# Full 128-by-128 products in the search for the experts' thresholds, and attention's state products moved behind its results

## The chip, the core and the metric

The kernel runs on one core of a Trainium2 chip. The metric is the device time of one execution in microseconds (us), the median of several runs. The core has a matrix engine (TensorE: PE for its products, PEld for the loading of the stationary operand), VectorE (DVE), ScalarE (ACT), GpSimd (POOL) and DMA queues. A product's form is written as rows*columns of the array that it uses: `128*48` takes a contraction over 128 rows and 48 output partitions. The shape behind it is that of the moving operand.

## What is computed

Three stages follow each other: a linear attention with a decaying state, a dense two-layer network with a squared ReLU, and a routed network of eight experts with a fixed capacity of N/E = 384 tokens each.

```python
for t in range(S):                                   # attention, B=4, H=8, S=768, D=48
    state = alpha[:, :, t, :, None] * state + einsum('bhd,bhe->bhde', k[:, :, t], v[:, :, t])
    y[:, :, t] = einsum('bhd,bhde->bhe', q[:, :, t], state)
x = y.transpose(0, 2, 1, 3).reshape(3072, 384)
h = maximum(x @ w_in, 0); x = h * h @ w_out          # dense, d_ff = 2048
logits = x @ w_gate                                  # routed, 8 experts, d_ff = 1024
# (token, expert) pairs in falling order of logit: a token takes the expert if both are still free
out[mask] = maximum(x[mask] @ w1[e], 0) @ w2[e]
```

## The kernel before

**Attention and the dense network.** The 3072 tokens are 24 chunks of 128 (six to each of the four batch rows), and three chunks make a unit of 384 for the dense network. Eight units run one behind the other, each in 16 steps `f`: `moe_a` (9 products into `ph`, line 388), the square on ACT, DVE and POOL (`moe_ev`, lines 393 to 404), and two steps later `moe_b` (9 products into three `p2` banks, line 416). Between these steps stand the pieces of one attention chunk each: `psc` (scores, line 252, form 48*128), `pn` (transposes, 292), and in the last piece the state's products `pu` (line 303, form 128*48) and the result's `py`, which are first those with the decayed state `sad` (line 270, form 112*128) and then those with the masked scores `Pt` (line 273, form 128*48). `update` makes `pu`, and DVE adds it to the state (line 309); the next chunk's `sad` is made of it on POOL. `result` makes `py`, and ACT copies it out (line 276). Chunks 0 and 1 run before the first unit, chunk 2 (`late`) has its update last. A chunk that begins a batch row has no `sad`, one that ends it (`last`) has no update. That leaves fourteen chunks from chunk 3 on with all three: 3, 4, 7 to 10, 13 to 16 and 19 to 22.

In the first unit DVE also converts the dense network's weights (`narrow`, lines 348 to 352), and the order on every engine is the program's. From the second unit on a scheduler places the instructions of the other engines by their readiness.

**The search.** An expert's threshold is found in five rounds (`it` 0 to 4) of a 32-way search. Each round is a chain between PE and DVE: `cm` (line 861, comparisons), six products `pc` (869, 128*128), a copy `rc` (872), four products `pb` with the constant `same` (882), a comparison `full` (885), one product with the constant `later` (887), its sum `n` (896), and the next `cm`. A last product `pz` (908) gives the counts. `same` has 32 columns for each product (form 128*32), `later` has 32 rows (32*128), and `pz` takes 32 rows (32*128): the 32 threshold candidates lie on 32 partitions. There are seven such searches, `k` = 0 to 6. Search 0 runs among the dense network's last unit (line 671), search 1 while the first expert's weights are prepared, and searches 2 to 6 inside the experts' products.

**The experts.** Each expert has eight steps `s`: `layer1` (9 products, line 988, with ACT's and DVE's lines 996 and 997 behind it) and `layer2` (three times 3 products, line 1006). A hand-written table (`STEADY`, `EXTRA` and others) says what is put before, between and behind them in each step: a piece of the search, a gather, `expert_x` (transposes, line 961, whose results ACT and DVE copy in 962 and 963), or the split of the next expert's weights into two parts (951 on ACT, 953 on POOL or DVE). What stands in the table is the order of the program, and of every engine's queue.

Of the kernel before, what the change touches and what calls it, by code (L numbers as in the profile page):

```python
# [7 lines left out]
F32 = mybir.dt.float32  # L8
F32R = mybir.dt.float32r
BF = mybir.dt.bfloat16  # L10
F16 = mybir.dt.float16
I32 = mybir.dt.int32
AF = mybir.ActivationFunctionType
OP = mybir.AluOpType
# [6 lines left out]
E, F2 = 8, 1024  # L21
# [3 lines left out]
CPU = 3  # L25
# [7 lines left out]
T = 32  # L33
G = 128 // T
ITERS = 5
# [50 lines left out]
def moe_kernel(ctx: ExitStack, tc: tile.TileContext, akq, v, w_in, w_out, w_gate, w1, w2, out,  # L86
               dbg=None, force=False):
    nc = tc.nc
    pe, dve, act, pool, sp = nc.tensor, nc.vector, nc.scalar, nc.gpsimd, nc.sync
    consts = ctx.enter_context(tc.tile_pool(name="consts", bufs=1))  # L90
# [40 lines left out]
    ident = consts.tile([128, 128], F32, name="ident")  # L131
    dve.tensor_scalar(ident, jp, 0.0, None, op0=OP.is_equal)
    ones = consts.tile([128, 128], F32, name="ones")
# [3 lines left out]
    scratch = consts.tile([128, 1], F32, name="scratch")  # L137
# [31 lines left out]
    for i in range(2):  # L169
        t = ap_.tile([112, NP, 128], F32, name=f"sad{i}")  # L170
# [6 lines left out]
    def iota(shape, pattern, base=0, cm=0, name="io"):  # L177
        t = consts.tile(shape, F32, name=name)
        pool.iota(t, pattern=pattern, base=base, channel_multiplier=cm, allow_small_or_imprecise_dtypes=True)
        return t  # L180

    ioe = iota([128, E], [[1, E]], base=ID0, name="ioe")
    iop = iota([128, 1], [[0, 1]], cm=1, name="iop")
# [2 lines left out]
    pool.iota(iopc[:, :, 1], pattern=[[1, NCH]], base=0, channel_multiplier=0, allow_small_or_imprecise_dtypes=True)  # L186
    onesb = consts.tile([128, 128], BF, name="onesb")
    trim = consts.tile([128, 128], BF, name="trim")
    later = consts.tile([T, 128], BF, name="later")
    same = consts.tile([128, 128], F16, name="same")  # L190
    iopw = iota([128, 1], [[0, 1]], base=-128 * ID0, cm=1, name="iopw")
    sel = consts.tile([16, E], F32, name="sel")

    def late_consts():
        pool.memset(onesb, 1.0)
        dve.tensor_scalar(trim, jp, 0.0, -1.0, op0=OP.is_gt, op1=OP.add)
        dve.tensor_scalar(later, ones[0:T], iop[0:T], 0.5, op0=OP.mult, op1=OP.is_gt)
        dve.tensor_copy(same, ident)
        dve.tensor_scalar(sel, jp[0:16, 0:E], -float(E), None, op0=OP.is_equal)
        dve.tensor_tensor(sel, sel, ident[0:16, 0:E], op=OP.add)  # L200

# [10 lines left out]
    def attn(ch, tags="aaaaa"):  # L212
# [3 lines left out]
        last = c == S // C - 1  # L216
# [31 lines left out]
        late = ch == CPU - 1  # L248
        for p in (3, 0, 1, 2) if late else range(NP):
            for j in range(2):  # L250
                o = 64 * j
                pe.matmul(psc[j][:, p * 128:(p + 1) * 128], kt[o:o + D, p], qt[o:o + D, p],  # L252
                          start=True, stop=True)
# [44 lines left out]
        def update():  # L298
            pu = bank(next(tag), "pu")
            for p in range(NP):  # L300
                for j in range(2):
                    o = 64 * j
                    pe.matmul(pu[o:o + D, p * 64:p * 64 + D], kn2[:, p, j], vn[:, 2 * p + j],  # L303
                              start=True, stop=True)
            for j in range(2):
                o = 64 * j
                src = v4(pu[o:o + D, 0:256])[:, :, 0:D]
                if c:
                    dve.tensor_tensor(state[o:o + D], src, sa[o:o + D, :, o:o + D], op=OP.add)  # L309
                else:  # L310
                    (act.copy if ch == 0 else dve.tensor_copy)(state[o:o + D], src)

        if not (last or late):
            update()
        result(0, NP - late)
        if late:
            update()
        yield "o"

# [370 lines left out]
    sm, sm_stack = open_pool("route", "right")  # L690
# [8 lines left out]
    cap = sm.tile([128, E], F32, name="cap")  # L699
# [7 lines left out]
    pool.iota(iot[:, 0], pattern=[[1, T]], base=0, channel_multiplier=0, allow_small_or_imprecise_dtypes=True)  # L707
    for i in range(1, ITERS):
        act.activation(iot[:, i], iot[:, i - 1], AF.Copy, scale=1.0 / T)
    iol = sm.tile([T, 1], F32, name="iol")  # L710
    act.activation(iol, iop[0:T], AF.Copy, scale=float(T) ** (1 - ITERS))
    ioslot = sm.tile([128, CAP], F32, name="ioslot")
    pool.iota(ioslot, pattern=[[1, CAP]], base=-int(OFF), channel_multiplier=0, allow_small_or_imprecise_dtypes=True)
    IDX, XG, RW = {}, {}, {}
# [116 lines left out]
    def search(k):  # L831
# [20 lines left out]
        n, at = None, zero24[:, 0:1]  # L852
        for it in range(ITERS):

            pc = bank("a", "pc")
            thr = iot[:, 0]
            if it:
                thr = pc[:, G * E:G * E + T]
                dve.tensor_scalar(thr, iot[:, it], n, at, op0=OP.add, op1=OP.add)
            cm = sm.tile([128, NCH, T], BF, name="cm", bufs=2)  # L860
            dve.tensor_tensor(cm, m2[:, :, None].to_broadcast([128, NCH, T]),
                              thr[:, None, :].to_broadcast([128, NCH, T]), op=OP.is_ge)
            if it == 0:
                oh = sm.tile(eb, BF, name="oh", bufs=2)
                dve.tensor_tensor(oh, L, m[:, :, None].to_broadcast(eb), op=OP.is_equal)
            yield

            for c in range(0, NCH, G):
                pe.matmul(pc[:, 0:G * E], cm[:, c:c + G].rearrange("p c t -> p (c t)"),
                          oh[:, c:c + G].rearrange("p c e -> p (c e)"), start=c == 0, stop=c == NCH - G)  # L870
            rc = sm.tile([128, G * E], F16, name="rc", bufs=2)
            dve.tensor_copy(rc, pc[:, 0:G * E])
            if it == 1:
                ee = sm.tile(eb, F32, name="ee", bufs=1)
                dve.tensor_tensor(ee, oh, ioe[:, None, :].to_broadcast(eb), op=OP.mult)
            if it == 2:
                ei = sm.tile([128, NCH], F32, name="ei", bufs=2)
                dve.tensor_reduce(ei, ee, axis=AX.X, op=OP.add)
            yield
            pb = bank("a", "pb")  # L880
            for g in range(G):
                pe.matmul(pb[0:T, 0:E], same[:, g * T:(g + 1) * T], rc[:, g * E:(g + 1) * E], start=g == 0,
                          stop=g == G - 1)
            full = sm.tile([T, E], BF, name="full", bufs=2)
            dve.tensor_tensor(full, pb[0:T, 0:E], cap[0:T], op=OP.is_ge)
            yield
            pe.matmul(pb[:, E:2 * E], later, full, start=True, stop=True)
            if it == 1:
                at = n
            elif 1 < it < ITERS - 1:  # L890
                at2 = sm.tile([128, 1], F32, name="at", bufs=2)
                dve.tensor_scalar(at2, at, n, None, op0=OP.add)
                at = at2
            n0, n = n, sm.tile([128, 1], F32, name="n", bufs=4)
            steps = sm.tile([128, E], F32, name="steps", bufs=1)
            dve.tensor_scalar(steps, pb[:, E:2 * E], float(T) ** -it, None, op0=OP.mult, op1=OP.max, accum_out=n)
            yield

        hi = sm.tile([128, 1], F32, name="hi", bufs=2)
        dve.tensor_scalar(hi, n, n0, at, op0=OP.add, op1=OP.add)  # L900
        taken = sm.tile([T, E], F32, name="taken", bufs=2)
        dve.scalar_tensor_tensor(taken, n[0:T].to_broadcast([T, E]), iol, pb[0:T, 0:E], op0=OP.is_equal, op1=OP.mult)
        a = pb[:, 2 * E:2 * E + NCH]
        dve.tensor_scalar(a, m2, hi, None, op0=OP.is_ge)
        dve.copy_predicated(aid, a.bitcast(mybir.dt.uint32), ei)
        yield
        pz = bank("a", "pz")
        pe.matmul(pz[:, 0:E], ones[0:T], taken, start=True, stop=True)
        cl = sm.tile([128, E], F32, name="cl", bufs=2)
        dve.tensor_tensor(cl, cap, pz[:, 0:E], op=OP.subtract)  # L910
        cz = sm.tile([128, E], F32, name="cz", bufs=2)
# [379 lines left out]
```

## Time and profile before

| | |
|---|---|
| median of three runs | 868.7 us (868.61 to 869.08) |
| the profiled execution | 867.91 us |
| its span in the trace | 865.7 us |
| PE busy | 813.1 us, 94% of the span |
| DVE, ACT, POOL busy | 498.1, 337.6, 366.3 us |
| granted clock of PE, mean | 0.975 |

The profiled execution's time is 2.2 us more than its span, which is what lies around the trace. The trace is read here by its timeline: a row stands for a run of equal instructions on one engine, and the difference of the starts of two neighbouring rows is what the first of them took of the engine, since PE's own ends are modelled. Tenths of a microsecond in such differences are the subject of this case.

### The profile page before, as it was taken

What the parts mean: (1) busy time and instruction counts of PE and PEld (TensorE: products, weight loads), DVE (VectorE), ACT (ScalarE), POOL (GpSimd) and SP (SyncE); (2) the same over time, 40 slices, a digit from 0 to 9 for tenths busy, and PEclk for the clock granted to TensorE, in tenths of its full rate; (3) what the DMA queues carried; (4) which work ended last, traced back from release to release, by engine and by line L of the source; (5) the groups of instructions that cost most, each with busy time, mean ns of one, the idle gap of its engine ahead of it and who ended that gap; (6) DMA issues with size and microseconds to landing.
All of it is one profiled execution on the core that took longest, in us unless ns stands there. A gap on an engine that the chain in (4) does not pass through costs nothing.

```text
span 865.7 us, 14472 instructions
## 1 busy us (share of the span) xinstructions
PE 813.1 (94%) x5752; PEld 755.0 (87%) x5752; DVE 498.1 (58%) x1149; ACT 337.6 (39%) x615; POOL 366.3 (42%) x350
## 2 busy tenths in 40 slices
PE   7699999999999999999999999986999999999994
PEld 6588898999999999999999998875887888889993
DVE  7999884444444434435434213476876877876730
ACT  2265464233234233233233334213435536536620
POOL 2456562343342343343242344125457567572511
PEclk9899899999999999999999999996999999999997
DMA  8545322112112112112100000031432522513500
GB/s 257 158 160 188 125 76 79 42 49 69 43 49 70 42 49 70 42 49 74 64 23 28 1 23 13 15 143 49 173 129 74 201 97 105 192 69 141 199 31 30
DMA packets 21626, 75.54 MB, mean 87 GB/s; under 512 B 3137, under 2 KB 10178, under 8 KB 19634
## 3 DMA queue, kind: packets, MB, share of 16 engines
q0 software_dynamic: 5520, 34.61, 10.9%
q1 hardware_dynamic: 11682, 25.72, 9.4%
q10 hardware_dynamic: 4352, 14.24, 5.5%
q8 instruction: 46, 0.75, 0.4%
q14 instruction: 26, 0.21, 0.1%
HBM read 63.84 MB, written 9.54 MB: 85 GB/s over the span
## 4 chain that ended last, share of the span: by engine, by line
PE 76%; DVE 11%; ACT 5%; DMA 3%; issue 2%; POOL 0%; SPq 0%; POOLq 0%; DVEq 0%; ACTq 0%
PE ph L388 22%; PE p L416 20%; PE ph L988 9%; PE py L1006 7%; ACT wbuf L951 3%; PE psc L252 3%; DVE wbuf L953 3%; PE py L273 2%; PE p L671 2%; PE py L270 2%; DMA akq<-in_akq_dram 2%; DMA w1s<-in_moe_w_dram,wi 2%; PE pn L292 1%; DVE hl L997 1%; PE pu L303 1%
## 5 line engine op out<-in xcount | busy, mean ns | idle before, releaser
L388 PE MATMUL ph<-xT,wbuf 128*128 128x384 f32 x1152 | 228.3, 342 | 7.2 <-DVE wbuf L459 5.0
L388 PEld LDWEIGHTS ph<-xT,wbuf 128*128 128x128 f32 x1152 | 206.1, 190 | 10.9 <-DVE wbuf L459 6.0
L416 PE MATMUL p<-wbuf,hl 128*128 128x392 f32 (+1 forms) x1008 | 204.1, 346 | 0.0
L400 DVE SCALAR_TENSOR_TENSOR s<-ph,s 128x384 f32<-128x384 f32 x112 | 62.3, 557 | 223.4 <-ACT s L393 222.9
L416 PEld LDWEIGHTS p<-wbuf,hl 128*128 128x128 f32 x1008 | 177.8, 189 | 4.0 <-issue 3.0
L404 POOL TENSOR_TENSOR hl<-s,hl 128x384 fp32r<-128x384 f32 x96 | 97.6, 1017 | 184.3 <-ACT hl L401 176.3
L393 ACT ACTIVATE s<-ph 128x384 f32<-128x384 f32 x128 | 63.1, 493 | 175.7 <-PE ph L388 138.9
L1006 PE MATMUL py<-wbuf,hl 128*128 128x384 f32 x576 | 125.3, 348 | 0.0
L988 PE MATMUL ph<-xt,wbuf 128*128 128x384 f32 x576 | 118.4, 349 | 1.4 <-DVE xt L963 0.9
L988 PEld LDWEIGHTS ph<-xt,wbuf 128*128 128x128 f32 x576 | 100.2, 190 | 4.7 <-DVE xt L963 2.3
L1006 PEld LDWEIGHTS py<-wbuf,hl 128*128 128x128 f32 x576 | 99.0, 188 | 0.7
L401 ACT ACTIVATE hl<-s 128x384 fp32r<-128x384 f32 x96 | 50.4, 525 | 73.6 <-DVE s L400 73.6
L996 ACT ACTIVATE hl<-ph 128x384 fp32r<-128x384 f32 x64 | 31.8, 497 | 114.1 <-PE ph L988 110.4
L997 DVE SCALAR_TENSOR_TENSOR hl<-ph,hl 128x384 fp32r<-128x384 f32 x64 | 35.5, 555 | 35.0 <-ACT hl L996 35.0
L951 ACT ACTIVATE wbuf<-w1s 128x1024 fp32r<-128x1024 f32 x24 | 52.2, 2221 | 2.5 <-DMA w1s<-in_moe_w_dram,wi 2.5
L1014 POOL DMA_INDIRECT out_dram<-o,idx x24 | 28.6, 1193 | 50.9 <-ACT o L1011 19.8
L953 POOL TENSOR_TENSOR wbuf<-w2s,wbuf 128x768 fp32r<-128x768 f32 x24 | 43.5, 1837 | 6.0 <-ACT wbuf L951 6.0
L245 POOL TENSOR_TENSOR sad<-state,ae 48x192 f32<-48x192 f32 x40 | 25.1, 628 | 37.7 <-DVE state L309 28.6
L759 POOL DMA_INDIRECT xg<-x2d,row x24 | 23.0, 957 | 38.9 <-DVE idx L815 14.9
L356 POOL TENSOR_TENSOR wbuf<-wf,wbuf 128x384 fp32r<-128x384 f32 x16 | 21.1, 1322 | 37.9 <-ACT wbuf L355 37.9
L225 DVE TENSOR_TENSOR_SCAN suf<-akq,fresh 112x516 f32<-112x516 f32 x24 | 31.8, 1325 | 4.9 <-DMA akq<-in_akq_dram 4.4
L953 POOL TENSOR_TENSOR wbuf<-w1s,wbuf 128x1024 fp32r<-128x1024 f32 x11 | 32.9, 3014 | 3.0 <-ACT wbuf L951 2.9
(211 smaller groups left out, 1091.0 us busy)
## 6 DMA issues: line engine op xcount, KB each, us to landing
akq<-in_akq_dram ACTq DMA_DIRECT2D x16, 677.2 KB, 4.5
rawi<-in_moe_w_in_dram SPq DMA_DIRECT2D x16, 384.0 KB, 3.3
rawo<-in_moe_w_out_dram SPq DMA_DIRECT2D x16, 384.0 KB, 3.9
akq<-in_akq_dram SPq DMA_DIRECT2D x7, 677.2 KB, 5.6
x2d<-xo SPq DMA_DIRECT2D x24, 192.0 KB, 2.0
v<-in_v_dram ACTq DMA_DIRECT2D x16, 192.0 KB, 2.4
v<-in_v_dram SPq DMA_DIRECT2D x8, 192.0 KB, 6.9
xf<-xf SPq DMA_DIRECT2D x16, 72.0 KB, 2.6
```

Source lines behind the costliest of these rows:

```text
L225: dve.tensor_tensor_scan(back(one(P)), back(one(al)), back(one(fresh)), 1.0, op0=OP.mult, op1=OP.add)
L388: pe.matmul(ph[:, :UT], win[:, wi, kt, fs], XT[u][:, xi, kt, :], start=n == 0, stop=n == 3 * KT - 1)
L393: act.activation(s, ph[:, :UT], AF.Relu)
L400: dve.scalar_tensor_tensor(s, ph[:, :UT], 0.0, s, op0=OP.max, op1=OP.mult)
L401: act.activation(hl[:, 0], s, AF.Copy)
L404: (dve if u == 0 or (u, f) == (NU - 1, FT - 1) else pool).tensor_tensor(hl[:, 1], s, hl[:, 0].bitcast(F32), op=OP.subtract)
L416: pe.matmul(PY[u][t][:, :w], hl[:, si, t * C:(t + 1) * C], wout[:, wi, f, :w], start=f == 0 and n == 0, stop=f == FT - 1 and n == 2)
L951: act.activation(dst[:, 0], src, AF.Copy)
L953: (dve if "d" in e else pool).tensor_tensor(dst[:, 1], src, dst[:, 0].bitcast(F32), op=OP.subtract)
L988: pe.matmul(ph[:, :CAP], wa[:, wi, kt, j, :], xt[:, xi, kt, :], start=n == 0, stop=n == 3 * KT - 1)
L997: dve.scalar_tensor_tensor(hl[:, 1], ph[:, :CAP], 0.0, hl[:, 0].bitcast(F32), op0=OP.max, op1=OP.subtract)
L1006: pe.matmul(PX[k, i][:, :DM], hl[:, hi_, i * 128:(i + 1) * 128], wb[:, wi, j, :], start=j == 0 and n == 0, stop=j == FT2 - 1 and n == 2)
```

## The change

The four `same` products, the `later` product and `pz` use all 128 rows and columns: `same` repeats each of its 32 columns four times, so that the candidates' counts stand on all partitions, and `later` is zero outside its first 32 rows. `same` is now made by one POOL copy at the beginning of the routing stage, `later` by three DVE instructions instead of one, and `full`, `taken` and `iol` have 128 partitions. In attention the update goes behind the result from chunk 2 on; chunks 0 and 1 keep the old order.

```diff
-    later = consts.tile([T, 128], BF, name="later")
-    same = consts.tile([128, 128], F16, name="same")
+    later = consts.tile([128, 128], BF, name="later")
...
-        dve.tensor_scalar(later, ones[0:T], iop[0:T], 0.5, op0=OP.mult, op1=OP.is_gt)
-        dve.tensor_copy(same, ident)
+        dve.tensor_scalar(scratch, iop, 0.5, None, op0=OP.is_gt)
+        dve.scalar_tensor_tensor(scratch, iop, T - 0.5, scratch, op0=OP.is_lt, op1=OP.mult)
+        dve.tensor_scalar(later, ones, scratch, None, op0=OP.mult)
...
-        if not (last or late):
+        if ch < CPU - 1:
             update()
         result(0, NP - late)
-        if late:
+        if ch >= CPU - 1 and not last:
             update()
...
+    same = sm.tile([128, G, 128], F16, name="same")
+    pool.tensor_copy(same.rearrange("p g (r t) -> p g r t", t=T),
+                     ident.rearrange("p (g t) -> p g t", g=G)[:, :, None, :].to_broadcast([128, G, 128 // T, T]))
...
-                pe.matmul(pb[0:T, 0:E], same[:, g * T:(g + 1) * T], rc[:, g * E:(g + 1) * E], start=g == 0,
+                pe.matmul(pb[:, 0:E], same[:, g], rc[:, g * E:(g + 1) * E], start=g == 0,
                           stop=g == G - 1)
-            full = sm.tile([T, E], BF, name="full", bufs=2)
-            dve.tensor_tensor(full, pb[0:T, 0:E], cap[0:T], op=OP.is_ge)
+            full = sm.tile([128, E], BF, name="full", bufs=2)
+            dve.tensor_tensor(full, pb[:, 0:E], cap, op=OP.is_ge)
...
-        pe.matmul(pz[:, 0:E], ones[0:T], taken, start=True, stop=True)
+        pe.matmul(pz[:, 0:E], ones, taken, start=True, stop=True)
```

**PE, last piece of chunk 14** (`p_2677` to `p_2679` are the unit's three banks of `moe_b`). Before:

```order
L388 MATMUL ph<-xT,wbuf_64 128x384 x9
L303 MATMUL pu<-v_79,kn_2964 48x48 x8
L270 MATMUL py<-qt,sad_102 128x128 x4
L273 MATMUL py<-Pt,v_79 48x128 x8
L416 MATMUL p_2677<-wbuf_65,hl 128x392 x3
L416 MATMUL p_2678<-wbuf_65,hl 128x392 x3
L416 MATMUL p_2679<-wbuf_65,hl 128x392 x3
L388 MATMUL ph<-xT,wbuf_64 128x384 x9
```

Now:

```order
L389 MATMUL ph<-xT,wbuf_64 128x384 x9
L271 MATMUL py<-qt,sad_102 128x128 x4
L274 MATMUL py<-Pt,v_79 48x128 x8
L304 MATMUL pu<-v_79,kn_2964 48x48 x8
L417 MATMUL p_2677<-wbuf_65,hl 128x392 x3
L417 MATMUL p_2678<-wbuf_65,hl 128x392 x3
L417 MATMUL p_2679<-wbuf_65,hl 128x392 x3
L389 MATMUL ph<-xT,wbuf_64 128x384 x9
```

The products with `sad` stand directly behind `moe_a`, and the two runs with 48 columns behind each other. Chunks 3 and 4, in the first unit, are turned in the same way.

**DVE, the instructions around the addition of chunk 14's `pu`** (`s<-ph,s` is the square of `moe_ev`, `qt` the next chunk's scaled queries). Before:

```order
L229 SCALAR_TENSOR_TENSOR A<-akq_75,whole 112x515
L309 TENSOR_TENSOR state<-pu,sad_102 48x192 x2
L400 SCALAR_TENSOR_TENSOR s<-ph,s 128x384
L234 TENSOR_TENSOR qt<-akq_75,A 112x512
L400 SCALAR_TENSOR_TENSOR s<-ph,s 128x384 x5
```

Now:

```order
L230 SCALAR_TENSOR_TENSOR A<-akq_75,whole 112x515
L235 TENSOR_TENSOR qt<-akq_75,A 112x512
L401 SCALAR_TENSOR_TENSOR s<-ph,s 128x384
L310 TENSOR_TENSOR state<-pu,sad_102 48x192 x2
L401 SCALAR_TENSOR_TENSOR s<-ph,s 128x384 x5
```

The addition goes behind the next chunk's `qt` and one square. In the first unit, where the order is the program's, DVE's additions for chunks 3 and 4 keep their places.

**PE, one round of the search inside an expert** (`py_5896`, `py_5900`, `py_5917` are the expert's three banks of `layer2`, `ph_6091` is that of `layer1`). Before, from the last of the four `same` products on:

```order
L882 LDWEIGHTS same
L882 MATMUL pb<-rc,same 32x8
L1006 MATMUL py_5896<-wbuf_64,hl_5949 128x384 x3
L1006 MATMUL py_5900<-wbuf_64,hl_5949 128x384 x3
L1006 MATMUL py_5917<-wbuf_64,hl_5949 128x384 x3
L887 LDWEIGHTS later
L887 MATMUL pb<-full,later 128x8
L988 MATMUL ph_6091<-xt,wbuf_64 128x384 x9
```

Now:

```order
L887 LDWEIGHTS same
L887 MATMUL pb<-rc,same 128x8
L1011 MATMUL py_5898<-wbuf_64,hl_5951 128x384 x3
L1011 MATMUL py_5902<-wbuf_64,hl_5951 128x384 x3
L1011 MATMUL py_5919<-wbuf_64,hl_5951 128x384 x3
L892 LDWEIGHTS later
L892 MATMUL pb<-full,later 128x8
L993 MATMUL ph_6093<-xt,wbuf_64 128x384 x9
```

Nothing moves here; the output of `same` has 128 partitions instead of 32.

## Rows read from the trace of the kernel before

**Rows 1.** Busy time by stretch: PE, PEld, DVE, ACT, POOL, then clock, DMA.
```profile
140.00:480.00 340.00, 339.90 (x2455) 324.60 (x2456) 145.27 (x240) 115.95 (x238) 119.11 (x144) 1.00 0.16 50
92.00:98.00 6.00, 6.00 (x24) 6.00 (x24) 6.00 (x13) 2.97 (x7) 2.61 (x3) 0.50 0.55 183
```

**Rows 2.** Timeline of PE, chunk 14's last piece (start us, us, line, form).
```profile
303.02 1.75 PE L388 MATMUL ph<-xT,wbuf 128*128 128x384 f32 x9
304.70 0.56 PE L303 MATMUL pu<-v,kn 128*48 128x48 f32 x16
305.20 1.16 PE L270 MATMUL py<-qt,sad 112*128 112x128 f32 x8
...
309.01 1.75 PE L388 MATMUL ph<-xT,wbuf 128*128 128x384 f32 x9
```

**Rows 3.** The same of chunk 11, which has no update.
```profile
240.40 1.75 PE L388 MATMUL ph<-xT,wbuf 128*128 128x384 f32 x9
...
245.69 1.74 PE L388 MATMUL ph<-xT,wbuf 128*128 128x384 f32 x9
```

**Rows 4.** The same of chunk 12, which has no sad.
```profile
264.97 0.56 PE L303 MATMUL pu<-v,kn 128*48 128x48 f32 x16
265.37 1.05 PE L273 MATMUL py<-Pt,v 128*48 128x128 f32 x16
```

**Rows 5.** Timeline of PE, search 3, rounds 3 and 4, inside an expert.
```profile
662.54 0.77 PE L1006 MATMUL py<-wbuf,hl 128*128 128x384 f32 x3
663.24 0.25 PE L882 MATMUL pb<-rc,same 128*32 128x8 f16 x4
663.42 0.55 PE L961 MATMUL px<-ident,xg 128*128 128x128 f32 x3
663.73 0.76 PE L1006 MATMUL py<-wbuf,hl 128*128 128x384 f32 x3
664.42 0.17 PE L887 MATMUL pb<-full,later 32*128 32x8 bf16 x1
664.53 1.83 PE L988 MATMUL ph<-xt,wbuf 128*128 128x384 f32 x9
666.20 0.69 PE L1006 MATMUL py<-wbuf,hl 128*128 128x384 f32 x3
666.73 0.32 PE L869 MATMUL pc<-oh,cm 128*128 128x32 bf16 x6
666.89 0.78 PE L1006 MATMUL py<-wbuf,hl 128*128 128x384 f32 x3
```

**Rows 6.** Weight loads by form from 540 to 780 us: busy us, mean ns.
```profile
L869 PEld LDWEIGHTS <-cm 128*128 128x128 bf16 x210 | 7.9, 98 | 13.5 <-DVE cm L861 10.9 <-issue 1.9 <-DVE idx L815 0.5
L882 PEld LDWEIGHTS <-same 128*32 128x32 f16 x140 | 6.4, 94 | 12.0 <-issue 11.7
```

**Rows 7.** Timeline of PE: two waits of search 3.
```profile
657.73 0.32 PE L869 MATMUL pc<-oh,cm 128*128 128x32 bf16 x6 [0.61 <-DVE cm L861]
...
672.82 0.17 PE L766 MATMUL pp<-mi,onesb 128*128 128x24 bf16 x1 [0.27 <-DVE wi L735]
```

**Rows 8.** The chain that ended last (start us, us, what), in search 3.
```profile
648.84 3.73 ACT wbuf L951 x2
```

**Rows 9.** Timeline of DVE: the comparisons of round 4, search 3.
```profile
665.67 0.95 DVE L861 TENSOR_TENSOR cm<-m,pc 128x768 bf16<-128x768 f32 x1
```

**Rows 10.** Timeline of DVE in the first unit: chunks 3 and 4.
```profile
50.01 0.73 DVE L309 TENSOR_TENSOR state<-pu,sad 48x192 f32<-48x192 f32 x2
...
77.63 0.74 DVE L309 TENSOR_TENSOR state<-pu,sad 48x192 f32<-48x192 f32 x2 [0.93 <-PE pu L303]
...
81.79 0.56 DVE L404 TENSOR_TENSOR hl<-ph,hl 128x384 fp32r<-128x384 f32 x1 [0.88 <-ACT hl L401]
```

**Rows 11.** Timeline of PE in the first unit.
```profile
48.00 0.56 PE L303 MATMUL pu<-v,kn 128*48 128x48 f32 x16
...
90.03 2.18 PE L388 MATMUL ph<-xT,wbuf 128*128 128x384 f32 x9 [1.90 <-DVE wbuf L459]
```

More of the change, by code (lines that the diff above doesn't have):

```diff
@@ L709, in moe_kernel @@
         act.activation(iot[:, i], iot[:, i - 1], AF.Copy, scale=1.0 / T)
-    iol = sm.tile([T, 1], F32, name="iol")
-    act.activation(iol, iop[0:T], AF.Copy, scale=float(T) ** (1 - ITERS))
+    iol = sm.tile([128, 1], F32, name="iol")
+    same = sm.tile([128, G, 128], F16, name="same")
+    pool.tensor_copy(same.rearrange("p g (r t) -> p g r t", t=T),
+                     ident.rearrange("p (g t) -> p g t", g=G)[:, :, None, :].to_broadcast([128, G, 128 // T, T]))
+    act.activation(iol, iop, AF.Copy, scale=float(T) ** (1 - ITERS))
     ioslot = sm.tile([128, CAP], F32, name="ioslot")
@@ L900, in search @@
         dve.tensor_scalar(hi, n, n0, at, op0=OP.add, op1=OP.add)
-        taken = sm.tile([T, E], F32, name="taken", bufs=2)
-        dve.scalar_tensor_tensor(taken, n[0:T].to_broadcast([T, E]), iol, pb[0:T, 0:E], op0=OP.is_equal, op1=OP.mult)
+        taken = sm.tile([128, E], F32, name="taken", bufs=2)
+        dve.scalar_tensor_tensor(taken, n.to_broadcast([128, E]), iol, pb[:, 0:E], op0=OP.is_equal, op1=OP.mult)
         a = pb[:, 2 * E:2 * E + NCH]
```

## The prediction

> **What bounds the kernel now.** I read the busy times by stretch first. From 140 to 480 us PE is busy for 339.9 of 340 us at the full clock [rows 1]: there the product engine is the bound, and every tenth that one of its steps loses or wins moves the end. Next comes the timeline of PE, where the difference of two starts is a step's cost. In chunk 14's last piece 5.99 us pass from one `moe_a` to the next [rows 2]; in chunk 11's, which has the same products but for `pu`, 5.29 us [rows 3] (between the two rows shown stand L270 x8, L273 x16 and L416 x9). So the sixteen `pu` instructions cost 0.70 us there. In chunk 12, where `pu` is followed by `Pt` products of the same form, it takes 0.40 us [rows 4], and in chunk 14, where it is followed by the 112*128 form, 0.50 us [rows 2]. What is lost belongs to the changes of form, not to the products.
>
> The experts' stage shows the same. Three `layer2` products take 0.53 us ahead of `pc`, which has the full form (666.20 to 666.73), but 0.70 us ahead of `pb` and 0.69 us ahead of `later` [rows 5]. Here PE is not alone, though: it waits 0.61 us for `cm` at round 2 of search 3 and 0.27 us at its end [rows 7], and the chain that ended last runs over ACT's weight splits at 648.84 [rows 8]. In the first unit DVE is the bound: PE waits 1.90 us for it at 90.03 [rows 11].
>
> **The change part by part.** *Attention from the second unit on.* With `pu` behind `Pt`, the piece is chunk 11's plus a `pu` without a change of form on one of its sides: 5.29 + 0.40 = 5.69 us against 5.99, so 0.30 us less [rows 2 to 4]. Twelve of the fourteen chunks lie in this stage: 12 x 0.30 = 3.6 us, all on the path. The three chunks that begin a batch row have no `sad`, and only swap two runs of one form: nothing. What is moved later is the state: `pu` comes 1.8 us later, but the order puts one square and the next chunk's `qt` ahead of DVE's addition now, and the next reader, that chunk's `sad` products, stands some 20 us away; DVE works 145 of 340 us here [rows 1]. Zero for that. Bounds for the term: 3.0 (an exit from `pu` dearer than one from `Pt`) and 4.2.
>
> The Trainium skill (TensorEngine Tiling (Array Packing), Tiling Modes, key properties) says that a change of tiling mode drains TensorE, and its TensorE: Matmul & The Clock Gate (Part 2, step 4) gives a drain of about 128 cycles, which I estimate at 0.053 us; two changes fewer would then give 0.11 us a piece and 1.3 us in all. The rows show 0.30, and the sum keeps to them.
>
> *Chunks 3 and 4.* There the order is the program's, and DVE's addition waits for `pu` in front of all conversions. PE now makes `sad` and `Pt` first, 1.9 us together. For chunk 3, `pu` began at 48.00 and would end at about 48.00 + 1.85 + 0.56 = 50.4; DVE reaches the addition at 50.01 without idle time [rows 10, 11]: 0.4 us lost on DVE. For chunk 4, DVE already waits for `pu` (0.93 us), so it starts 1.8 us later, of which its later idle 0.88 us, for ACT, can take back about as much [rows 10]: 0.9 us lost. Both reach PE through the wait at 90.03. Term: +1.3 us instead of a gain of 0.6. Bounds: -0.5 (if the slow-clock stretch that follows this wait, 92 to 98 at 0.50 [rows 1], is not entered) and +2.5.
>
> *Searches 2 to 6.* A `pb` group costs 0.70 - 0.53 = 0.17 us ahead of it and 0.18 us itself (663.24 to 663.42); four products of the full form at `pc`'s pace (six in 0.16 us) would take 0.11, so it gains 0.17 + 0.07 = 0.24 us. `later` costs 0.16 ahead and 0.11 itself, of which 0.03 remain: also 0.24 us [rows 5]. Five searches have 25 of each. Not all of that is kept. Rounds 0 and 1 end in the 0.61 us wait [rows 7], behind a chain of ACT's splits and DVE's work that no PE product starts [rows 8]: their four groups, 0.96 us, only lengthen it to some 1.5 us. In round 2 `full` stands on DVE behind the copy of the first transposes, and I keep 0.22 of 0.48. In round 3 the comparisons of round 4 end at 665.67 + 0.95 = 666.62, and `pc` starts at 666.73 [rows 5, 9]: a slack of 0.11 us, so `pc` can only follow what the second transposes win, which is `pb`'s 0.24. Round 4 keeps nearly all, 0.44. Together 0.9 us a search, 4.5 us in all. Bounds: 0.5 a search (2.5) and 1.4, all of rounds 2 to 4 (7.0). `pz` is absorbed by the 0.27 us wait [rows 7].
>
> *Searches 0 and 1.* By the same prices: in search 0 three of the five `pb` groups follow a filler without a wait (0.13 each, less where `pc` slows the filler anyway), every `later` gives 0.08 to what follows it, and `pz` some 0.25: 1.0 us. In search 1 PE mostly waits for DVE: 0.2 us. Bounds together 0.4 and 2.0.
>
> *The rest is nothing.* `same` is one POOL copy some 7 us ahead of its first use, on an idle queue; if that cover were gone it would cost about a microsecond, once. The two more instructions for `later` are a column wide. `full` and `taken` get more partitions, not longer rows. The loads of `same` become four times as wide: `pc`'s loads, 128 columns, take 98 ns, those of `same`, 32 columns, 94 ns [rows 6]. That is 4 ns for 140 loads, under 0.6 us if none is hidden, and I take zero.
>
> The Trainium skill (TensorE: Matmul & The Clock Gate, LDWEIGHTS (loading the stationary operand)) gives a load time of columns over 1.2, so 128 columns against 32 would add an estimated 80 ns to each of the 140 loads, 11 us in all. The two rows do not agree with it for 16-bit weights.
>
> Sum: -3.6 + 1.3 - 4.5 - 1.2 = -8.0 us. The profiled execution, 867.9 us, becomes 859.9. It lies 0.8 us under the median of the runs, so the median becomes 860.7.
>
> **The rivals.** *All of it is kept* (853.7): the waits shrink with the products, because the chain behind them starts earlier as well. Then 50 groups x 0.23 = 11.5 us from the searches, 1.2 from the first two, 3.6 from attention, less 1.3. Against it: the ACT splits on the chain [rows 8] start behind a `layer1` product that lies ahead of the round.
>
> *The gaps are not the form's* (866.4): in the searches PE would have waited for `rc` and `full` all along, and only attention's 3.6 - 1.3 remain. For it: every group there is released by DVE. Against it: the filler ahead of `pb` and `later` costs the same 0.16 to 0.17 us extra in both places, and attention shows the effect without DVE.
>
> *The clock falls in the longer waits* (875.7, slower). The waits of searches 2 to 6 grow from about 0.6 to 1.5 us. The 1.90 us wait at 90.03 [rows 11] is followed by a stretch at half clock, 0.50 from 92 to 98 [rows 1], in which PE loses at least 3.0 us. If each of the five waits did that, it would be 860.7 + 15.0. It decides from three such stretches on (9.0 us against the 8.0 gained). Against it: the trace has two more waits of that length in its first 141 us at full clock, and none as short as 1.5 us that lowered it.
>
> *Wider loads cost their width* (877, slower). Four times 94 ns is 376 [rows 6], 282 ns more for each load; 60 of them lie in rounds 2 to 4, where PE is the bound: 16.9 us. Against it stands the 98 ns of `pc`'s loads.
>
> **How the numbers follow.** The forecast has 0.66; its own range, from the bounds of the terms without taking all ends at once, is 856.5 to 864.5. All kept: 0.11. Not the form's: 0.12. The clock: 0.06. Wider loads: 0.02. Another, unnamed: 0.03. A range of 855.5 to 866.8 takes in the forecast and the third case and leaves out some 0.2. About 0.2% (1.7 us) is what a measurement of this kernel can tell from no change, so faster means below 867.0. Forecast and all kept are faster, the third case mostly so: 0.87. Same: 0.07. Slower: 0.06.
>
> **What would show it.** In the profile after: chunk 14's piece at 5.7 us between its two `moe_a`; `layer2`'s three products ahead of `pb` and `later` at 0.53 to 0.6 us; the wait for `cm` at round 2 grown to about 1.5 us at full clock; DVE idle for about 2 us ahead of chunk 4's addition, and PE's wait near 90 us grown to about 3 us. It would be wrong if PE waited for DVE in the attention stage, if the wait near 90 us were gone, or if a search of the experts' stage kept 0.2 us or 2 us.

## The result, and the profile after

The changed kernel takes 860.1 us (median of 4 runs, 856.3 to 863.3) beside 868.75 us of the kernel before: 0.9898 of its time, with an interval of 0.9857 to 0.9939. The forecast was 860.7. In a second comparison the same kernel took 857.97 us (6 runs, 856.8 to 864.0) beside 870.0 (11 runs, 866.8 to 874.6): 0.9871, from 0.9838 to 0.9905. The profiled execution lasts 860.50 us, 7.4 less than before; its span is 858.7 us, 7.0 less. The sum of the prediction had said 8.0, but several of its terms were wrong by more than a microsecond and cancelled each other.

The timeline of PE in chunk 14's last piece answers to [rows 2]. Columns: start us, us, engine, line, what.

```profile
300.75 1.75 PE L389 MATMUL ph<-xT,wbuf 128*128 128x384 f32 x9
302.33 1.05 PE L271 MATMUL py<-qt,sad 112*128 112x128 f32 x8
303.31 1.08 PE L274 MATMUL py<-Pt,v 128*48 128x128 f32 x16
304.23 0.53 PE L304 MATMUL pu<-v,kn 128*48 128x48 f32 x16
304.68 1.87 PE L417 MATMUL p<-wbuf,hl 128*128 128x392 f32 x9
306.39 1.74 PE L389 MATMUL ph<-xT,wbuf 128*128 128x384 f32 x9
```

From `moe_a` to `moe_a` 5.64 us pass instead of 5.99. Step by step: `moe_a` 1.58 us (1.68 before), `sad` 0.98 (1.08), `Pt` 0.92 (1.02), `pu` 0.45 (0.50), `moe_b` 1.71 as before. The 112*128 form behind the full form costs `moe_a` nothing; the form with 48 columns did.

Rounds 2 to 4 of search 3, PE again, answer to [rows 5, 7].

```profile
653.16 0.32 PE L874 MATMUL pc<-oh,cm 128*128 128x32 bf16 x6 [1.26 <-DVE cm L866]
...
657.32 0.32 PE L874 MATMUL pc<-oh,cm 128*128 128x32 bf16 x6
657.48 0.53 PE L966 MATMUL px<-ident,xg 128*128 128x128 f32 x3
657.77 0.76 PE L1011 MATMUL py<-wbuf,hl 128*128 128x384 f32 x3
658.38 0.26 PE L887 MATMUL pb<-rc,same 128*128 128x8 f16 x4
658.49 0.53 PE L966 MATMUL px<-ident,xg 128*128 128x128 f32 x3
658.77 0.77 PE L1011 MATMUL py<-wbuf,hl 128*128 128x384 f32 x3
659.39 0.18 PE L892 MATMUL pb<-full,later 128*128 128x8 bf16 x1
659.43 1.83 PE L993 MATMUL ph<-xt,wbuf 128*128 128x384 f32 x9
661.09 0.69 PE L1011 MATMUL py<-wbuf,hl 128*128 128x384 f32 x3
661.74 0.32 PE L874 MATMUL pc<-oh,cm 128*128 128x32 bf16 x6
...
664.95 0.69 PE L1011 MATMUL py<-wbuf,hl 128*128 128x384 f32 x3
665.48 0.28 PE L913 MATMUL pz<-taken,ones 128*128 128x8 f32 x2
...
667.87 0.17 PE L771 MATMUL pp<-mi,onesb 128*128 128x24 bf16 x1 [0.95 <-DVE wi L740]
```

Three `layer2` products now take 0.61 us ahead of `pb` and 0.62 ahead of `later` (0.70 and 0.69 before), `pb` itself 0.11 (0.18) and `later` 0.04 (0.11). The three products still take 0.53 us ahead of `pc` where it doesn't wait for `cm` (656.79 to 657.32, in round 3), and now 0.53 ahead of `pz`, where they took 0.62. `pz` before:

```profile
670.29 0.69 PE L1006 MATMUL py<-wbuf,hl 128*128 128x384 f32 x3
670.91 0.38 PE L908 MATMUL pz<-taken,ones 32*128 32x8 f32 x2
```

But PE waits 1.26 us for `cm` where it waited 0.61, and 0.95 us ahead of `pp` where it waited 0.27.

To see what each stage kept I set marks on PE's timeline (the starts of `pn` and of `pc`) and compared the stretches between them. Each number is the difference of two starts, in us.

| stretch | before | after | predicted | measured |
|---|---|---|---|---|
| start to chunk 3's transposes | 43.12 | 43.43 | 0 | +0.3 |
| chunk 3's to chunk 6's transposes | 88.14 | 87.98 | +1.3 | -0.2 |
| chunk 6's to chunk 7's transposes | 22.71 | 22.24 | 0 | -0.5 |
| attention from there to search 0 | 400.28 | 395.69 | -3.6 | -4.6 |
| search 0 | 28.48 | 27.75 | -1.0 | -0.7 |
| search 1 | 30.74 | 32.21 | -0.2 | +1.5 |
| searches 2 to 6 and the end | 239.07 | 235.98 | -4.5 | -3.1 |

Chunk 5 ends a batch row and has no transposes; where an expectation below says chunk 5's, the mark is chunk 6's, and where it says chunk 23's, it is chunk 22's. The stretches sum to -7.3. Behind the start of PE's last product the span is 0.3 us longer, and what lies around the trace is 0.5 us shorter (1.8, 2.2 before); that makes the 7.4. The start and search 1 vary from trace to trace in one kernel, and the first unit goes with a stretch at half clock that some traces have, as the experiments show. The other four stretches together keep 8.9 us.

### The profile page after: what moved, and what is told of

Same layout as the page of the kernel before. It is cut to its first block, busy times and chain, and to the rows that moved or that the text cites. A ratio compares the mean times of both kernels' runs of the same rounds, so it can differ in the third digit from the quotient of the medians.

```text
span 858.7 us, 14480 instructions
## 1 busy us (share of the span) xinstructions
PE 799.7 (93%) x5752; PEld 753.1 (88%) x5752; DVE 499.2 (58%) x1150; ACT 339.5 (40%) x615; POOL 368.1 (43%) x351
## 4 chain that ended last, share of the span: by engine, by line
PE 76%; DVE 14%; DMA 3%; ACT 3%; issue 2%; POOL 0%; SPq 0%; POOLq 0%; DVEq 0%; ACTq 0%
PE ph L389 22%; PE p L417 20%; PE ph L993 10%; PE py L1011 8%; DVE wbuf L958 3%; PE py L274 3%; PE psc L253 2%; PE p L672 2%; PE py L271 2%; DMA w1s<-in_moe_w_dram,wi 2%; ACT wbuf L956 2%; DMA akq<-in_akq_dram 2%; PE pn L293 1%; DVE suf L226 1%; DVE hl L1002 1%
## 5 line engine op out<-in xcount | busy, mean ns | idle before, releaser
L1019 POOL DMA_INDIRECT out_dram<-o,idx x24 | 30.5, 1270 | 52.0 <-ACT o L1016 18.4
L246 POOL TENSOR_TENSOR sad<-state,ae 48x192 f32<-48x192 f32 x40 | 27.0, 675 | 47.6 <-DVE state L310 36.9
L357 POOL TENSOR_TENSOR wbuf<-wf,wbuf 128x384 fp32r<-128x384 f32 x16 | 18.3, 1141 | 37.3 <-ACT wbuf L356 37.2
```

## The experiments

The first four kernels ran on one chip, the next four on a second and the last three on a third; each time is given with that of the kernel before beside it, or compared within its four.

**The two parts alone.** The first kernel has the change of attention only, the second that of the search only:

```diff
-        if not (last or late):
+        if ch < CPU - 1:
             update()
         result(0, NP - late)
-        if late:
+        if ch >= CPU - 1 and not last:
             update()
```

```diff
-                pe.matmul(pb[0:T, 0:E], same[:, g * T:(g + 1) * T], rc[:, g * E:(g + 1) * E], start=g == 0,
+                pe.matmul(pb[:, 0:E], same[:, g], rc[:, g * E:(g + 1) * E], start=g == 0,
...
-        pe.matmul(pz[:, 0:E], ones[0:T], taken, start=True, stop=True)
+        pe.matmul(pz[:, 0:E], ones, taken, start=True, stop=True)
```

> The kernel before with the new order of attention's update alone. Theory (the two parts add, as the trace after reads): pieces with state and result at 5.64 us between their two moe_a instead of 6.00, twelve times, so 4.3 us, and about 0.9 us more at the unit's and the row's boundaries; the first unit gains or loses up to 1.3 us with its slow-clock stretches; nothing in the searches. 863.6 us, between 861.5 and 866. Rival (what attention wins is given back behind it, because the searches wait for something else): 868 or more. Rival (the change of the search's forms is what shortened attention's stage too, by other places in memory): pieces stay at 6.00.

> The kernel before with the full forms of the search alone, attention's order as before. Theory: pieces at 6.00 as before; searches 2 to 6 each 0.6 to 0.75 us shorter (3.1 us together), search 0 shorter by 0.7; 864.9 us, between 863 and 867, with search 1's slow-clock stretches (586 to 600 before) as the part that can move by 1.5 us. Rival (all of the groups' gain is kept): 856. Rival (nothing is kept, the waits grow by all of it): 868.7.

Attention alone took 865.4 us (12 runs, 862.2 to 869.5) beside 869.6 (23 runs, 866.4 to 877.9): 0.9954, from 0.9927 to 0.9982. The search alone took 867.3 (12 runs, 864.7 to 870.2): 0.9965, from 0.9943 to 0.9988; it was expected between 863 and 867, a miss by 0.3. Each part is a gain by itself. The spread of the runs is larger than the parts, so the stretches tell more. From chunk 7's to chunk 22's transposes: 317.54 before, 317.52 with the search alone, 313.32 with attention alone, 313.31 with both. Search 0: 28.48 and 28.50 with the old forms, 27.73 and 27.75 with the full ones. Searches 2 to 6 and the end: 239.1 and 239.0 with the old forms, 235.9 and 236.0 with the full ones. The parts don't touch each other, and nothing that attention wins is given back. Both rivals of the first expectation and both of the second fall. PE's timeline of the first kernel has chunk 14's piece in the new order, without any change in the search:

```profile
304.38 1.75 PE L388 MATMUL ph<-xT,wbuf 128*128 128x384 f32 x9
305.96 1.05 PE L270 MATMUL py<-qt,sad 112*128 112x128 f32 x8
...
307.86 0.53 PE L303 MATMUL pu<-v,kn 128*48 128x48 f32 x16
308.32 1.87 PE L416 MATMUL p<-wbuf,hl 128*128 128x392 f32 x9
310.03 1.22 PE L388 MATMUL ph<-xT,wbuf 128*128 128x384 f32 x6
```

310.03 - 304.38 = 5.65 us (the last row is cut by the window).

**The first unit in the old order.**

```diff
-        if ch < CPU - 1:
+        early = ch < CPU - 1 or ch in (CPU, CPU + 1)
+        if early:
             update()
         result(0, NP - late)
-        if ch >= CPU - 1 and not last:
+        if not (early or last):
             update()
```

> The changed kernel, but chunks 3 and 4 (the first unit) keep the update ahead of the result. Theory (the later pu costs DVE time there): DVE's addition of chunk 4 waits 0.9 us instead of 2.7, and the start of the second unit comes 0.5 to 1.3 us earlier than in the changed kernel, so 859 us. Rival (the first unit's end hangs on its slow-clock stretches, not on this wait): the start of the second unit within 0.3 us of that of the kernel before, and 860 or more.

858.0 us (6 runs, 856.6 to 859.5) beside the same 869.6. On DVE's timeline the addition of chunk 4 waits 0.93 us again, where the changed kernel has 2.69:

```profile
80.61 0.74 DVE L310 TENSOR_TENSOR state<-pu,sad 48x192 f32<-48x192 f32 x2 [0.93 <-PE pu L304]
```

```profile
80.08 0.74 DVE L310 TENSOR_TENSOR state<-pu,sad 48x192 f32<-48x192 f32 x2 [2.69 <-PE pu L304]
```

The start of the second unit, which the expectation names, can't be compared: the kernel's start alone took 46.4 us here and 43.4 in the changed kernel. The way from chunk 4's to chunk 6's transposes shows what this wait costs. In every kernel with the late `pu` it is 58.5 to 58.6 us, but for one trace at 57.96. With the early `pu` it is 57.7 to 57.9 where PE keeps its full clock, and 59.0 to 59.1 in the two traces of the kernel before, where the clock stands at 0.50 from 91 to 98. So the wait costs 0.6 to 0.9 us, as the theory has it. The stretch at half clock, the rival's cause, costs another 1.2; it entered two traces of six with the early `pu` and none of seven with the late one.

**Idle products in search 1.** Its length in the trace after was the largest surprise, so the next two kernels keep PE busy there. The first had the idle products twice too long for the waits, since one of them takes 0.23 us and not 0.11; the second is sized by it (`w` is one idle product, ones by ones).

```diff
-         "1 A t 99 t 1 s 1 t x h0 B r d0 h1 r d1 r h2 p2 r open r h3 r h4 p3 h5 r r r x h6 r p4 p5 r r r p6").split()
+         "1 A t 99 t 1 s 1 t x h0 B r d0 h1 r w w w w w w w w w w w w w w w w w w w w d1 r h2 p2 w w w w w w w w w w w w r w w w w w w w w w w w w open r h3 r h4 p3 h5 r r r x h6 r w w w w w w w w p4 p5 r r r p6").split()
```

```diff
-         "1 A t 99 t 1 s 1 t x h0 B r d0 h1 r d1 r h2 p2 r open r h3 r h4 p3 h5 r r r x h6 r p4 p5 r r r p6").split()
+         "1 A t 99 t 1 s 1 t x h0 B r d0 h1 r w w w w w w w w w w w d1 r h2 p2 w w w w w w w w r w w w w w w open r h3 r h4 p3 h5 r r r x h6 r w w w w w w w p4 p5 r r r p6").split()
```

> The changed kernel with 52 idle products of ones by ones (0.11 us each) put into PE's waits of search 1: 20 behind pc of round 0, 12 behind pb, 12 behind later, 8 behind pc of round 2. Theory (the idle waits of 2.7, 1.75 and 1.6 us lead to the two half-clock stretches 582 to 588 and 593 to 603, and these set search 1's length and most of the spread of the runs from 856 to 863): no half clock from 575 to 610, about 3 us less than the changed kernel, so 857 us, and runs within 1.5 us. Rival (DVE is the bound of search 1 and the half clock costs nothing): 860, within 0.5 us of the changed kernel.

> The changed kernel with the idle products in search 1 sized by the trace with too many of them, where one of them takes 0.23 us of PE: 11 behind pc of round 0, 8 behind pb, 6 behind later, 7 behind pc of round 2. Theory (half clock is what lengthens search 1): full clock from 574 to 610; search 1 at 27.7 us (30.7 before, 32.2 after), so 3 to 4.5 us less than the changed kernel beside it, about 857.5. Rival (DVE bounds search 1, so the clock only decides how long PE waits): search 1 at 30 us or more, and the time within 0.7 us of the changed kernel.

> The changed kernel once more, as the neighbour of the next two on one chip. Theory (attention and searches are fixed; the spread of the runs comes from the start of the kernel and from search 1's half clock): from attention's chunk 7 to chunk 23 313.3 us as in the first trace; search 0 27.7; searches 4 and 5 32.6 each; search 1 anywhere from 29.3 to 32.8, the first 42 us anywhere up to 47. About 861 us. Rival (the waits in the experts' stage vary too): searches 2 to 6 differ from the first trace by more than 0.5 us somewhere.

With too many 859.8 us (6 runs, 857.2 to 863.6), with the right number 858.2 (6 runs, 855.3 to 860.8), and the changed kernel beside the latter 858.0. The time tells nothing. The traces do: the clock is whole in both. With too many idle products search 1 takes 31.27 us, 10.4 of it in round 0 (6.8 in the changed kernel): there they hold it up themselves, and the first expectation fails. With the right number it takes 28.50 us. Busy time by stretch, first the sized kernel, then the changed one (us, PE, PEld, DVE, ACT, POOL, clock, DMA):

```profile
574.00:588.00 14.00, 11.56 (x103) 9.85 (x102) 10.07 (x23) 9.18 (x8) 10.90 (x7) 1.00 0.58 205
588.00:605.00 17.00, 15.27 (x115) 13.83 (x111) 14.03 (x61) 3.57 (x8) 6.52 (x5) 1.00 0.19 61
```

```profile
582.00:589.00 7.00, 4.64 (x30) 4.33 (x30) 3.74 (x12) 2.63 (x5) 7.00 (x4) 0.51 0.26 99
589.00:592.00 3.00, 1.43 (x18) 1.27 (x18) 2.69 (x11) 1.54 (x4) 2.58 (x2) 1.00 0.01 3
592.00:603.00 11.00, 9.92 (x52) 9.01 (x51) 5.64 (x25) 1.47 (x3) 0.44 (x1) 0.53 0.00 1
```

In the changed kernel two stretches at half clock, 6.8 and 10.2 us long, follow PE's waits of 2.74, 1.75 and 1.61 us in round 0. The second trace of it has one, of 10.2 us, and search 1 takes 29.52. (The rest of that trace is as expected: attention 313.32, search 0 27.74, and searches 2 to 6 within 0.4 us of the first trace, so its rival falls.) Over all ten traces without idle products, of either kernel, search 1 goes with its time at half clock: 29.3 us with 6.8 of it, 29.3 to 29.5 with 10.2, 30.7 to 31.0 with 13.7, 32.2 to 32.8 with 17.1, 33.6 with 23.9. So the theory holds that half clock lengthens search 1, but beside the second trace by 1.0 us and not by 3 to 4.5. The spread of the runs, 7.1 us in the changed kernel, isn't explained by it: with idle products it is still 5.5, and the first stretch (start to chunk 3's transposes) alone varies from 42.1 to 47.4 us over all the traces.

**Both together.** The sized idle products, and chunks 3 and 4 in the old order.

> The same idle products, and the update of chunks 3 and 4 ahead of the result again. Theory (DVE's longer wait for chunk 4's pu costs PE about 0.5 us in the first unit): the way from chunk 4's to chunk 5's transposes takes 57.9 us, not 58.5, and the time is 0.5 to 1 us under that of the kernel with the idle products alone: 857. Rival (the first unit's end does not depend on it): within 0.3 us.

858.8 us (6 runs, 854.8 to 861.5); its profiled span, 853.0 us, is the shortest of all, with search 1 at 28.16 and chunk 4's to chunk 6's transposes at 57.66. By the stretches it is the best version; by its runs it can't be told from the changed kernel, and I don't claim that it beats it.

**Only `same` in the full form.** `later` and `pz` have 32 rows again.

```diff
-            pe.matmul(pb[:, E:2 * E], later, full, start=True, stop=True)
+            pe.matmul(pb[:, E:2 * E], later[0:T], full[0:T], start=True, stop=True)
...
-        pe.matmul(pz[:, 0:E], ones, taken, start=True, stop=True)
+        pe.matmul(pz[:, 0:E], ones[0:T], taken[0:T], start=True, stop=True)
```

> The changed kernel with full forms for the four same products alone; later and pz have 32 rows again. Theory (each form's change has its own price, 0.24 us a group, paid in rounds 2 to 4): later's product again costs 0.69 us behind its three layer2 products and 0.11 itself; searches 4 and 5 take 32.6 + 3 x 0.24 = 33.3 less what the waits give back, so 32.9 to 33.3, against 32.6 with all and 33.35 with none. Rival (the gain came from the first change of form in a round alone): 32.6 to 32.7.

Search 4 took 33.40 us and search 5 32.98, but their first rounds vary (below), so the rounds behind are read by themselves, from `pc` to `pc`, and from the last `pc` to `pp`:

| | round 2 | round 3 | round 4 to `pp` | sum |
|---|---|---|---|---|
| before | 4.36 | 4.64 | 6.10 | 15.10 |
| `same` alone | 4.23 | 4.46 | 6.01 | 14.70 |
| all three | 4.14 | 4.42 | 5.72 | 14.28 |

These repeat within 0.03 us in the undisturbed searches. `same` keeps 0.40 us of a search, `later` and `pz` another 0.42: each change of form has its own price, and the rival falls. That is 0.82 us, of which rounds 0 and 1 take back 0.08 (8.97 us before, 9.05 after, searches 3 to 6).

**What absorbs rounds 0 and 1.** These two kernels leave out the subtraction that DVE makes behind `full` of round 1.

```diff
-EXTRA = ((4, 2, "h0"), (4, 4, "h1"), (5, 3, "d0 h2"), (6, 0, "h3"), (6, 3, "x0"), (6, 4, "p2 p1"), (7, 3, "x2 p3"),
+EXTRA = ((4, 2, "h0"), (4, 4, "h1"), (5, 3, "h2"), (6, 0, "h3"), (6, 3, "x0"), (6, 4, "p2 p1"), (7, 3, "x2 p3"),
```

> The changed kernel without DVE's part of the next experts' first weight split (the 128x1024 subtraction behind full of round 1, 2.2 us, in searches 2 to 6); the low parts of these weights are left out of the result. Theory (this instruction is what the new forms' gain of rounds 0 and 1 is lost behind): the wait for cm at round 2, 1.2 us in the trace after, is gone; from pc of round 0 to pc of round 2 7.85 us instead of 9.05 in searches 3 to 6. Rival (ACT's splits ahead of it hold the chain as long): a wait of 0.5 us or more stays, 8.4 us or more.

> The kernel before without the same subtraction, with the same part of the result left out. Theory: its wait of 0.62 us for cm at round 2 is gone, from pc of round 0 to pc of round 2 8.36 us instead of 8.98; with the other kernel's 7.85 the new forms then keep 0.5 us of rounds 0 and 1, where they kept nothing (8.98 before, 9.05 after). Rival (the forms gain nothing in rounds 0 and 1 even without the wait): both kernels within 0.15 us of each other.

They took 861.9 and 866.1 us, one run each; the kernel before took 872.5 beside them. The wait for `cm` is gone in both. From `pc` of round 0 to `pc` of round 2, searches 3 to 6 take 8.63, 9.45, 8.71 and 7.99 us with the full forms, and 8.77, 9.63, 8.95 and 8.30 with the old ones. The full forms now keep 0.14 to 0.31 us, where they kept nothing: part of the theory. But only search 6 comes near the 7.85 that I expected, and in the others PE waits at another place instead, 0.8 to 1.7 us. On DVE's timeline of the first kernel, search 4:

```profile
681.25 0.95 DVE L866 TENSOR_TENSOR cm<-m,pc 128x768 bf16<-128x768 f32 x1
684.60 0.19 DVE L877 CAST rc<-pc 128x32 f16<-128x32 f32 x1 [2.40 <-remote]
```

DVE stands idle for 2.40 us ahead of `rc`, which waits only for `pc`'s products. These had begun at 682.26, and the profile has the last of them end at 682.57; but PE's ends are modelled. The trace's semaphore records have PE's signal at 684.57, 0.03 us ahead of `rc`. In three searches of the first kernel and in all four of the second, `rc` of round 1 is late by 0.4 to 2.0 us, and each time PE's signal comes 0.02 to 0.03 us ahead of it; in the remaining one, search 3 of the first, `full` is late instead (PE waits 0.81 us for it). So DVE waits for PE here; what holds PE's signal up is not shown.

These two kernels therefore don't show what the rounds keep undisturbed. Behind `later` of round 1, where nothing is late, the way to the next `pc` takes 2.22 us with the full forms and 2.31 with the old ones. With the way up to `later` in the first traces of the changed kernel and the kernel before (5.48 and 5.89 us) that makes 7.70 and 8.20. By this estimate the full forms would keep the 0.5 us that I expected.

Where the gain of the two rounds goes in the changed kernel, the first traces show. DVE's timeline, round 1 of search 3, before (`pc` of round 0 at 648.78):

```profile
653.54 0.56 DVE L997 SCALAR_TENSOR_TENSOR hl<-ph,hl 128x384 fp32r<-128x384 f32 x1 [0.38 <-ACT hl L996]
654.01 0.14 DVE L885 TENSOR_TENSOR full<-pb,cap 32x8 bf16<-32x8 f32 x1
```

After (`pc` of round 0 at 644.04):

```profile
648.86 0.56 DVE L1002 SCALAR_TENSOR_TENSOR hl<-ph,hl 128x384 fp32r<-128x384 f32 x1 [0.60 <-ACT hl L1001]
649.33 0.15 DVE L890 TENSOR_TENSOR full<-pb,cap 128x8 bf16<-128x8 f32 x1
649.41 2.28 DVE L958 TENSOR_TENSOR wbuf<-w1s,wbuf 128x1024 fp32r<-128x1024 f32 x1
651.59 0.17 DVE L901 TENSOR_SCALAR_CACHE_REDUCE steps<-pb 128x8 f32<-128x8 f32 x1
```

`full` begins 5.23 us behind `pc` of round 0 before and 5.29 after. It stands behind `hl`, which waits for ACT, and ACT comes to its part behind the weight splits, as the rival has it. So the gain is lost in that wait already. The subtraction follows `full` at once and holds the sum (`steps`) and `cm` behind it, as the theory has it; that `later` comes 0.4 us earlier has no effect.

**The kernel before once more.**

> The kernel before once more. Theory (startup and search 1 differ from run to run in the kernel before too, the rest does not): attention's chunk 7 to 23 317.54 us, search 0 28.48, searches 3 to 6 33.3 each, within 0.1; search 1 between 29.5 and 33, the first 42 us between 42 and 47. Rival (search 1 is fixed in the kernel before and only the changed kernel spreads it): 30.74 within 0.2 us again.

874.8 us for the one run, beside 872.5 of another run of the same kernel. Attention 317.52, search 0 28.53, as before; search 1 took 33.63, with a clock of 0.52 from 586 to 611, so it varies in the kernel before as well. The other part of the theory was wrong: searches 3 to 5 took 33.9 to 34.6 us, not 33.3. All of it lies in rounds 0 and 1, where searches 3 to 6 took 9.6 to 10.3 us instead of 9.0, with `rc` late by 1.0 to 1.8 in three of them, as in the kernels just shown.

## Why the prediction held

*Attention from the second unit on: right in kind, mis-sized.* A piece won 0.35 us, not 0.30: in every trace all twelve take 5.63 to 5.65 us with the late `pu` and 5.97 to 6.00 with the early one. The step that failed took [rows 4], 0.40 us, for `pu` without a change of form: that interval holds some of the entry into the form. With all else equal `pu` adds 5.64 - 5.29 = 0.35 us, so two changes of form cost 0.35. Twelve pieces make 4.2. The estimate of 0.11 us for two drains, worked out from the Trainium skill (TensorE: Matmul & The Clock Gate, Part 2, step 4), is a third of that.

*The swap of two runs of one form is "nothing": wrong by 0.8 us.* The pieces of chunks 12 and 18 indeed stay at 4.75 us, but the next two groups win 0.18 us each time, and the stretch around chunk 6 wins 0.47. Not PE's order does that, but DVE's: the state's copy now comes behind a square. At chunk 6 PE's wait for DVE's square falls from 1.90 us (at 140.10) to 1.43. Timeline of DVE at chunk 12, after:

```profile
264.70 0.69 DVE L235 TENSOR_TENSOR qt<-akq,A 112x512 f32<-112x512 f32 x1
265.31 0.55 DVE L401 SCALAR_TENSOR_TENSOR s<-ph,s 128x384 f32<-128x384 f32 x1
265.77 0.73 DVE L312 COPY state<-pu 48x192 f32<-48x192 f32 x2
```

Before, the square stood behind the copy, and with it all that followed, up to DVE's copy `L` out of the bank that `moe_b` needs next:

```profile
267.04 0.73 DVE L311 COPY state<-pu 48x192 f32<-48x192 f32 x2
267.80 0.56 DVE L400 SCALAR_TENSOR_TENSOR s<-ph,s 128x384 f32<-128x384 f32 x1
269.47 0.17 DVE L426 COPY L<-p 128x8 f32<-128x8 f32 x1 [1.11 <-ACT xo L424]
269.69 1.87 PE L416 MATMUL p<-wbuf,hl 128*128 128x392 f32 x9
```

So `moe_a` and `moe_b` there took 1.65 and 1.71 us instead of 1.58 and 1.60. The order shown for chunk 14 has the same move, and the prediction read it only as a delay of the state.

*Chunks 3 and 4: the wait for chunk 4 was right; the stage's -0.2 is luck.* DVE's addition for chunk 4 waits 2.69 us, as worked out (0.93 + 1.8). The one for chunk 3, for which the prediction had 0.4 us, waits for nothing (50.32, 6.89 us behind chunk 3's transposes, as before). PE's wait near 90 did not grow to 3 us; PE waited three times, which answers to [rows 11]:

```profile
85.83 1.85 PE L389 MATMUL ph<-xT,wbuf 128*128 128x384 f32 x9 [1.52 <-DVE wbuf L460]
...
91.28 1.85 PE L389 MATMUL ph<-xT,wbuf 128*128 128x384 f32 x9 [1.00 <-DVE wbuf L460]
...
97.22 1.85 PE L389 MATMUL ph<-xT,wbuf 128*128 128x384 f32 x9 [1.50 <-DVE wbuf L460]
```

No half clock follows these, while 6.8 us of it followed the 1.90 us before. But that is not the change's doing: with the early `pu` a wait of 1.90 to 1.91 us at the same place left the clock whole in four traces of six. Without half clock near 90, the way from chunk 3's to chunk 6's transposes takes 86.5 to 87.2 us with the early `pu` (four traces) and 86.9 to 88.1 with the late one (seven). In the means that is about 1.0 us more, so the +1.3 was not far off. The stage came out at -0.2 because the trace of the kernel before had the half clock; I had this as an end of the range (-0.5).

*Searches 2 to 6: the rounds came out right by two errors; the end and the accidents did not.* The step that failed priced a group at 0.24 us, because it took `layer2` ahead of `pc`, 0.53 us, for its time ahead of any full form. Ahead of the full `pb` and `later` it takes 0.61 to 0.62, just outside the 0.53 to 0.6 that were to show it. So the change of form costs 0.09 us ahead of a group and 0.07 in it, 0.16 together, and the other 0.08 stays; what that is, is not shown. Six groups make 0.96 us in rounds 2 to 4, not 1.44, and more of it is kept, 0.82, where the prediction kept 0.90 of its 1.44. Rounds 2 and 3 kept 0.22 each (predicted 0.22 and 0.24). Round 4 kept 0.38 of the 0.44, since the wait ahead of `pp` grew from 0.27 to 0.55 us: what I called absorbed for `pz` holds back part of the round as well. Rounds 0 and 1 lost 0.08 where I had nothing; that they keep nothing because of ACT's splits was right. The wait for `cm` grew from 0.6 to 1.2 us, by about four times 0.16, and not to 1.5. That makes 0.74 a search. Search 3 kept only 0.2, which the prediction had named as a sign of being wrong, because one small DVE instruction took 0.56 us instead of 0.17 on its way to `pp`, and search 2 kept 0.57.

```profile
666.42 0.08 DVE L917 DVE_READ_ACCUMULATOR cz<-cl 128x1 f32 x1
666.54 0.56 DVE L919 SCALAR_TENSOR_TENSOR ez<-cz,ioe 128x8 f32<-128x8 f32 x1
667.03 0.08 DVE L919 DVE_READ_ACCUMULATOR ez<-cz,ioe 128x1 f32 x1
```

*Search 0 and search 1.* Search 0 kept 0.7 of the 1.0. In search 1 the products' gain is small, as forecast, but the stretch became 1.5 us longer in the profiled execution with its half clock (17.1 us of it, 13.7 before). The step that failed gave this stage one value; it spreads by 3 to 4 us in either kernel (29.3 to 33.6 over all traces without idle products).

*The rivals.* "All of it is kept" and "the gaps are not the form's" fall by the table of rounds and by the kernel with `same` alone. Yet part of the second is true: 0.08 of the 0.17 us ahead of a group stay with the full form. "The clock falls in the longer waits" did not happen: the waits for `cm` in searches 2 to 6, 1.0 to 1.3 us long with all full forms, are at full clock in every trace; none of the forecast 1.5 us occurred. "Wider loads" falls: the loads of `same` take 97 ns on average in the trace after, 94 before [rows 6].

```profile
L887 PEld LDWEIGHTS <-same 128*128 128x128 f16 x140 | 6.9, 97 | 10.7 <-issue 10.5
```

The estimated 80 ns that the load rule of the Trainium skill (TensorE: Matmul & The Clock Gate, LDWEIGHTS (loading the stationary operand)) would add for columns four times as many are not there.

So the total was right partly by luck: between these two traces attention's gain was taken 1.0 us too small, with another 0.5 at chunk 6, and the first unit came out 1.5 better than forecast; the gain of searches 2 to 6 was taken 1.4 us too large, and search 1 went 1.7 the other way.

## What to carry to other kernels

Where the product engine never waits, the difference of the starts of two neighbouring groups, taken with and without one step, prices a change of form to a hundredth, and the gain adds up over the pieces. Where another engine's chain sets the pace, price the rounds one by one and expect part of the gain to come back as a wait. A price read as the difference of two places holds only if they differ in nothing else: here a third of it was not the form's. Compare fixed stretches of the traces when the runs spread by more than the effect, and look at what a scheduler did to the other engines' queues, too.

## What the runs showed of the hardware

- A change into and out of a form with 48 columns costs 0.35 us together, where the 112*128 form next to the full one cost `moe_a` nothing (1.58 us ahead of `sad`, 1.68 ahead of `pu`). In the search a group with 32 rows or 32 columns costs 0.09 us ahead of it and 0.07 in it.
- In the first unit waits of 1.5 us left the clock whole. One of 1.90 us near 90 was followed by 6.8 us at half clock in both traces of the kernel before, but in none of four other traces that have it.
- One DVE instruction of 0.17 us (`ez`) took 0.39 to 0.59 us in one or two of its seven executions in all nine traces of kernels with a full `same`, and in none of the four with the old forms. `rc` was late by up to 2.0 us because PE's signal for `pc` came that late behind its modelled end. The cause of both stays open.
